# A three-stage attention and MoE kernel: small routing operations on GpSimd, three more DMA transposes per pair, own places for V's scale and smaller zero-fill pieces

## The chip, the core and the metric

The kernel runs on one core of one Trainium2 chip. The metric is the device time of one execution in microseconds (us). Three executions of the kernel before took 1109.99, 1111.71 and 1105.46 us; their median is 1109.99 us. The engines are called as in the profile: PE is TensorE, DVE is VectorE, ACT is ScalarE, POOL is GpSimd, SP is SyncE, which here only issues DMAs.

## What is computed

The reference, cut to what matters, runs three layers one after the other on 4 batches of 576 tokens:

```python
# attention, 4 batches, 8 heads, 576 tokens, head size 64
scores = scale * q @ k.T
scores = where(scores >= max(scores) - tau, scores, -1e9)
attn = softmax(scores)
x = attn @ v                                   # 2304 tokens x 512
# MoE, 8 experts, one expert per token
logits = (x / |x|) @ (emb / |emb|).T / tau
idx = argmax(logits); gate = softmax(logits)[idx]
x = gate * (relu(x @ w1[idx]) @ w2[idx])
# dense layer
out = softplus(x @ w_in) @ w_out
```

## The kernel before, in words

**Phase A** is the attention and the routing of the tokens to their experts; it fills the first 400 us or so. Phases B (experts) and C (dense layer) follow, and the change leaves them alone.

Phase A works through 144 chunks, 36 to a batch: a chunk is 128 query rows of one head against all 576 keys (the last four chunks of a batch are two heads with 64 rows each). For a chunk n, PE makes the scores (`emit_s`, L284 and L287), DVE takes the row maximum (`emit_max`, L294) and the mask (`emit_mask`, L299), and ACT the exponential (`emit_exp`, L310). From there two chunks are handled as a **pair**: ACT rounds the exponentials to fp16 (`emit_hi`, L324), POOL makes the fp16 rest (`emit_lo`, L83 on tile PST). Both halves have to be transposed before PE can multiply them by V: 18 blocks of 128 x 128 per pair. 10 of them go by one DMA transpose that SP issues (L335), 8 over PE into a PSUM bank (`emit_half`, L349), from where ACT and DVE copy them out in turn (`emit_land`, L357 and L359). Then PE multiplies by V (`emit_pv`, L382) and DVE scales the result (`emit_evac`, L398 to L408).

The order of the work is written out by hand. Every operation gets a time in steps, one step per chunk, the list is sorted by that time, and the instructions are issued in this order; each engine runs its own in order. `emit_s` of chunk n stands at step n, the DMA transpose of its pair at n + 3.7, the product with V at n + 10.8. Other work is put between by the same clock:

- **V's scale** (L220 to L247). The next batch's V is split in two fp16 parts after a scale by its largest value. ACT takes maxima (`max_v`, L208), PE turns them (`prep_v0`, L220), DVE makes a factor (`prep_v1`), PE spreads it over the partitions (`prep_vb`, L242), DVE copies it out (`prep_vc`, L247). Then ACT and POOL make the two parts head by head (`prep_v2` L256/L258, `prep_v3` L83 on tile vl). `prep_v0` and `prep_vb` use one PSUM bank, called xt, together with the routing's transposes (`route_t` L430, evacuated by `route_x` L440) and logits (`route_l` L451, `route_c` L456). The places are VP + 0.95 to VP + 2.18 with VP = 30.
- **Routing** (`inv_norm` L85 to L108, `route_pick`, `route_gate`, `route_rank`). The operations on 128 x 5 and 128 x 40 elements of one batch run as a Python generator that moves on by one operation each half step, some 20 steps in all, beside the next batch's chunks. All of them are on DVE but the exponential. At its end POOL scatters the 5 token tiles into the buckets in HBM (`route_out`, L567). The last batch is routed in a tail after the 144 chunks, whose order is a string of words (DRAIN).
- **Zero fill** (`zero_fill`, L151). The 8 expert buckets are filled with zeros from a zero tile in SBUF, one DMA of 645 KB from 64 partitions per expert, on SP's queue, every 5 steps from step 20.

Of the kernel before, what the change touches and what calls it, by code (L numbers as in the profile page):

```python
# [44 lines left out]
DRAIN = """P8 g0 a1 z1 l2 a1 H2 a1 a1 H1 D3 a1 t5 P7 P6 a1 t4 D1 u5 L2 t3 a1 P5 c2 z1 p0 b1 V9 b1 a1 u4 a1 u3 P4 b1 t1 V5 b1 z1 b1 u1 t2 a1 u2 a1 z1 b1 z1 z1 a1 P3 r3 b1 b1 a1 x3 q3 b1 P2 V3 a1 b1 a1 g1 d1 d1 a1 P1 V1 l3 d1 r4 g2 d1 c3 q4 p1 d1 x4 d1 e1 f1 d1 e1 l4 f1 d1 e1 f1 e1 f1 d1 f1 e1 c4 z1 d1 e1 p2 h1 d1 e1 f1 d1 e1 f1 h1 a1 d1 e1 f1 h1 d1 f1 h1 f1 h1 f1 h1 d1 e1 d1 e1 e1 f1 h1 h1 e1 f1 d1 e1 f1 d1 e1 h1 d1 f1 f1 h1 e1 d1 d1 h1 d1 h1 e1 d1 e1 f1 h1 d1 e1 f1 h1 h1 e1 f1 f1 h1 d1 f1 h1 d1 e1 f1 e1 e1 f1 d1 f1 d1 e1 d1 h1 e1 h1 b1 h1 a1 z1 b1 z1 f1 b1 h1 a1 z1 b1 e1 e1 e1 b1 a1 a1 a1 d1 e1 b1 e1 d1 d1 e1 d1 e1 d1 d1 e1 d1 d1"""  # L45
QK0, QKD, V0, VD, VP, VS, Z0, ZD = 12, 7, 15, 3, 30, 2, 20, 5
DQ, DZ, VG = (0, 0, 0, 0), 1, 1
# [13 lines left out]
def attention_moe_moe_kernel(ctx: ExitStack, tc, qT, kT, v, tau, emb, moe_tau, w1, w2, wi, wo, out):  # L61
# [20 lines left out]
    def combine(eng, out, a, b, op):  # L82
        eng.tensor_tensor(out=out, in0=a, in1=b, op=op)  # L83

    def inv_norm(r, ss, t):  # L85
# [64 lines left out]
    def zero_fill(zeros, e, i):  # L150
        (act, sp)[DZ].dma_start(out=bucket[e * NT:e * NT + CAP].rearrange("(p r) c -> p r c", r=ZR)[64 * i:64 * i + 64],  # L151
                      in_=zeros.unsqueeze(1).to_broadcast([64, ZR, ROW]))

    def phase_a():
        with ExitStack() as es:
# [312 lines left out]
            def route_pick(b, t0, t1):  # L468
# [35 lines left out]
            def route_rank(b, t0, t1, eq, oh, shift):  # L504
# [35 lines left out]
            def route_gate(b, t0, t1):  # L540
# [17 lines left out]
                dve.tensor_scalar(out=gt, in0=gt, scalar1=1e-9, scalar2=None, op0=ALU.add)  # L558
                yield
# [111 lines left out]
            def at(n, fn, *a):  # L671
                work.setdefault(n, []).append((fn, a))
# [3 lines left out]
            def soon(t, fn, *a):  # L676
                late.append((t, fn, a))
# [627 lines left out]
```

## Time and profile before

| | before |
|---|---|
| median of three executions | 1109.99 us |
| the profiled execution | 1109.21 us, span 1107.5 us |
| PE busy | 993.5 us, 90% |
| DVE busy | 733.4 us, 66% |
| ACT busy | 619.0 us, 56% |
| POOL busy | 548.6 us, 50% |
| mean granted TensorE clock | 0.957 of full speed |

The busy shares are means over three phases with different limits. How the time of phase A is spent can be read from windows (busy time of each engine in a chosen stretch), from the list of waits, and from the timeline. Times are counted from the start of the span.

### The profile page before, as it was taken

Reading aid. Unit: us, or ns where it says so; the run is one execution under the profiler, and the core shown is the slowest. Engines: PE = TensorE matmul, PEld = TensorE weight load, DVE = VectorE, ACT = ScalarE, POOL = GpSimd, SP = SyncE. Lnnn points to the kernel's source line nnn. Section 1 sums busy time; section 2 is a strip of 40 time slices with the busy share of each in tenths; the row PEclk is TensorE's granted clock in tenths of the full one; section 3 lists DMA queues with packets and bytes.
Section 4 is the critical chain, followed back from the end, with each engine's and each line's share of the span. In section 5 each row is a group of like instructions: output and inputs, shape, how many; then the busy total and the mean of one; then the engine's idle time right before and its main releaser. Section 6 shows DMA issues by size and latency. Waiting matters only on the chain. (4 is left out here: it accounts for less than half of the span.)

```text
span 1107.5 us, 19252 instructions
## 1 busy us (share of the span) xinstructions
PE 993.5 (90%) x7314; PEld 849.9 (77%) x7314; DVE 733.4 (66%) x1432; ACT 619.0 (56%) x1070; POOL 548.6 (50%) x426
## 2 busy tenths in 40 slices
PE   6777887988798869999999998988899999999997
PEld 4665765767676658999999897766688888898996
DVE  7876897789689874766776558888533443544543
ACT  6776966878596743444444434444544544444543
POOL 4644646555564721656445442211555565565652
PEclk9888998999899978999999999899999999999999
DMA  5675987457443646887878866421100010010000
GB/s 153 130 155 118 165 164 150 97 115 139 113 91 63 129 131 201 206 225 212 207 204 183 194 181 129 152 76 39 50 26 1 29 39 1 29 39 1 29 1 29
DMA packets 155462, 121.73 MB, mean 110 GB/s; under 512 B 102360, under 2 KB 127960, under 8 KB 155360
## 3 DMA queue, kind: packets, MB, share of 16 engines
q1 hardware_dynamic: 136416, 93.16, 37.0%
q10 hardware_dynamic: 16032, 17.78, 6.4%
q0 software_dynamic: 2912, 9.48, 2.3%
q8 instruction: 59, 0.97, 0.4%
q14 instruction: 43, 0.35, 0.1%
HBM read 75.05 MB, written 20.01 MB: 86 GB/s over the span
## 5 line engine op out<-in xcount | busy, mean ns | idle before, releaser
L83 POOL TENSOR_TENSOR PST<-E,PST 128x1152 f16<-128x1152 f32 (+1 forms) x74 | 169.8, 2296 | 169.8 <-ACT PST L324 111.7
L1185 PE MATMUL a<-wo,g 128*128 128x512 f32 x864 | 218.3, 399 | 9.4 <-DVE g L83 9.4
L1157 PE MATMUL ch_ps<-cxt,wi 128*128 128x512 f32 (+1 forms) x960 | 214.7, 372 | 5.2 <-DVE cxt L83 3.2
L1157 PEld LDWEIGHTS ch_ps<-cxt,wi 128*128 128x128 f32 x960 | 177.3, 190 | 34.6 <-DVE cxt L83 3.5
L1185 PEld LDWEIGHTS a<-wo,g 128*128 128x128 f32 x864 | 162.2, 189 | 49.0 <-DVE g L83 13.7
L83 POOL TENSOR_TENSOR t<-e,t 128x512 f32<-128x512 f32 (+1 forms) x78 | 92.8, 1189 | 203.5 <-DVE t L1169 203.5
L284 PE MATMUL S<-k,qz 128*128 128x288 f32 x512 | 163.1, 444 | 19.8 <-DVE ss L98 7.0
L294 DVE TENSOR_SCALAR_CACHE_REDUCE Sb<-S,tau_s 128x576 f32<-128x576 f32 x144 | 116.6, 810 | 60.8 <-PE S L284 35.7
L1169 DVE TENSOR_SCALAR t<-e 128x512 f32<-128x512 f32 (+1 forms) x80 | 33.7, 421 | 157.6 <-ACT e L1167 157.6
L932 PE MATMUL h_ps<-xt,w 128*128 128x320 f32 x768 | 128.9, 316 | 5.1 <-ACT w L791 2.3
L83 POOL TENSOR_TENSOR w<-st,w 128x1024 fp32r<-128x1024 f32 x30 | 73.5, 2450 | 118.0 <-ACT w L791 116.1
L1166 ACT ACTIVATE e<-ch_ps 128x512 f32<-128x512 f32 (+1 forms) x80 | 44.1, 551 | 154.2 <-PE ch_ps L1157 154.2
L948 PE MATMUL y<-h,w 128*128 128x320 f32 x768 | 123.2, 310 | 0.0
L932 PEld LDWEIGHTS h_ps<-xt,w 128*128 128x128 f32 x768 | 115.0, 189 | 9.6 <-DVE w L83 3.8
L284 PEld LDWEIGHTS S<-k,qz 128*128 128x128 f32 x512 | 92.0, 200 | 39.2 <-issue 14.8
L299 DVE SCALAR_TENSOR_TENSOR Sb<-S,th,Sb 128x576 f32<-128x576 f32 x144 | 117.8, 818 | 5.1
L948 PEld LDWEIGHTS y<-h,w 128*128 128x128 f32 x768 | 115.8, 189 | 0.0
L382 PEld LDWEIGHTS <-PT 128*128 128x128 f16 (+1 forms) x2240 | 89.9, 104 | 24.2 <-issue 4.9
L310 ACT ACTIVATE E<-Sb,nb 128x576 f32<-128x576 f32 x144 | 103.8, 768 | 6.6 <-POOL PST L83 0.4
L382 PE MATMUL pv<-vh,PT 128*128 128x65 f16 (+1 forms) x1440 | 98.1, 199 | 6.1 <-DMA vh<-vh 3.5
L83 POOL TENSOR_TENSOR g<-g,t 128x512 f32<-128x512 f32 (+1 forms) x62 | 87.0, 1404 | 4.9
L791 ACT ACTIVATE w<-st 128x1024 fp32r<-128x1024 f32 x64 | 67.5, 1055 | 34.3 <-DMA st<-in_w 24.1
(166 smaller groups left out, 1438.0 us busy)
## 6 DMA issues: line engine op xcount, KB each, us to landing
st<-in_w SPq DMA_DIRECT2D x64, 512.0 KB, 5.2
raw<-in_wi SPq DMA_DIRECT2D x16, 512.0 KB, 4.7
raw<-in_wo SPq DMA_DIRECT2D x16, 512.0 KB, 3.3
bucket<-qz SPq DMA_DIRECT2D x8, 645.0 KB, 6.1
yT<-y ACTq DMA_DIRECT2D x7, 640.0 KB, 9.0
vst<-in_v ACTq DMA_DIRECT2D x12, 320.0 KB, 3.7
xr<-bucket SPq DMA_DIRECT2D x7, 516.0 KB, 5.8
k<-in_kT ACTq DMA_DIRECT2D x12, 288.0 KB, 2.9
```

The lines of the kernel that those rows point to most:

```text
L83: eng.tensor_tensor(out=out, in0=a, in1=b, op=op)
L284: pe.matmul(st[:, f, 0:HALF], q[:, h // 2, o:o + 128], k[:, h // 2, fs])
L294: dve.tensor_scalar(out=Sb[n], in0=St[n][:, :, 0:HALF], scalar1=tau_s[:, 0:1], scalar2=None, op0=ALU.subtract, op1=ALU.max, accum_out=TH[g ...
L299: dve.scalar_tensor_tensor(out=Sb[n], in0=St.pop(n)[:, :, 0:HALF], scalar=TH[g][:, j:j + 1], in1=Sb[n], op0=ALU.is_lt, op1=ALU.subtract)
L310: act.activation(out=Et[g][:, i].rearrange("p (f k) -> p f k", f=2), in_=Sb.pop(g * GS + i), func=ACTF.Exp, scale=-SCALE, bias=nb[:, i:i + 1])
L382: pe.matmul(oo, l, r, start=(z == 0), stop=(z == len(mms) - 1))
L791: act.activation(out=hi, in_=src, func=ACTF.Copy)
L932: pe.matmul(hps[:, 0:CAP], a[:, c, 128 * (f % 2):128 * (f % 2) + 128], b[:, c], start=(z == 0), stop=(z == 11))
L948: pe.matmul(Y[e][c][:, 0:CAP], a[:, f % 2, 128 * c:128 * c + 128], b, start=(f == 0 and z == 0), stop=(f == 7 and z == 2))
L1157: pe.matmul(h, a[:, r:r + 128], x[:, c, 0:n], start=(z == 0), stop=(z == 11))
L1166: act.activation(out=e, in_=h, func=ACTF.Abs)
L1185: pe.matmul(A[b][t], a[:, 128 * t:128 * t + 128], x, start=(f == 0 and z == 0), stop=(f == 15 and z == 2))
```

## The change

It has five parts.

- Of a pair's 18 blocks 13 now go by DMA (NDMA) and 5 over PE; the copy out of PSUM is 640 columns instead of 1024.
- For the first three batches most of the small routing operations move from DVE to POOL. `inv_norm_pool` takes the place of `inv_norm`; where one DVE instruction did two operations, POOL needs two instructions: 17 POOL instructions per batch stand for 13 on DVE. Where another engine takes the result up, 5 half steps (PLAG) are put between, so that a batch's routing lasts 18 half steps longer.
- V's scale: the load of V moves from steps 15, 18, 21, 24 to 14, 16, 18, 20, the maxima from 22 to 28 to 17 to 23, and the scale's own four operations from 30.95, 31.18, 31.95, 32.18 to 26.05, 27.18, 28.85, 29.18. The two parts of V start at step 30 instead of 34.
- Zero fill in 32 pieces of 161 KB, each from 16 partitions, from step 12, every 1.5 steps.
- POOL's order at the end of phase A: as the routing lasts longer, the third batch's scatters come later.

```diff
-NDMA, TLAG = 10, 6
-RKY, RKZ, VM, VMD = 2, 3, 22, 2
-QK0, QKD, V0, VD, VP, VS, Z0, ZD = 12, 7, 15, 3, 30, 2, 20, 5
+NDMA, TLAG = 13, 6
+PLAG = 5
+RKY, RKZ, VM, VMD = 2, 3, 17, 2
+QK0, QKD, V0, VD, VP, VS, Z0, ZD = 12, 7, 14, 2, 26, 2, 12, 1.5
...
+    def inv_norm_pool(r, ss, t):
+        dve.tensor_scalar(out=r.bitcast(U32), in0=ss.bitcast(U32), scalar1=1, scalar2=None,
+                          op0=ALU.logical_shift_right)
+        yield
+        dve.tensor_scalar(out=r.bitcast(U32), in0=r.bitcast(U32), scalar1=-1.0, scalar2=float(0x5F3759DF),
+                          op0=ALU.mult, op1=ALU.add)
+        yield
+        yield
+        combine(pool, t, r, r, ALU.mult)
+        combine(pool, t, t, ss, ALU.mult)
+        yield
+        pool.tensor_scalar(out=t, in0=t, scalar1=-0.5, scalar2=1.5, op0=ALU.mult, op1=ALU.add)
+        combine(pool, r, t, r, ALU.mult)
...
+        pool.tensor_scalar(out=t, in0=t, scalar1=1e-6, scalar2=None, op0=ALU.add)
+        for _ in range(PLAG):
+            yield
+        dve.reciprocal(out=r, in_=t)
...
     def zero_fill(zeros, e, i):
-        ...[64 * i:64 * i + 64], in_=zeros.unsqueeze(1).to_broadcast([64, ZR, ROW]))
+        ...[16 * i:16 * i + 16], in_=zeros.unsqueeze(1).to_broadcast([16, ZR, ROW]))
...
-                pt = HT[g] = pr.tile([128, 1024], F16, tag="T", name="T")
+                pt = HT[g] = pr.tile([128, 1024], F16, tag="T", name="T")[:, 0:128 * (18 - NDMA)]
...
-                yield from inv_norm(nrm, SS[b][0:R, t0:t1], tmp)
+                yield from (inv_norm_pool if b < B - 1 else inv_norm)(nrm, SS[b][0:R, t0:t1], tmp)
...
+                side = pool if b < B - 1 else dve
...
-                    dve.tensor_tensor(out=lg, in0=lg, in1=mx.unsqueeze(2).to_broadcast(bc), op=ALU.subtract)
+                    side.tensor_tensor(out=lg, in0=lg, in1=mx.unsqueeze(2).to_broadcast(bc), op=ALU.subtract)
...
+                if side is pool:
+                    pool.tensor_scalar(out=eq, in0=lg, scalar1=0.0, scalar2=None, op0=ALU.is_ge)
+                    combine(pool, eq, eq, iota, ALU.mult)
...
-                    dve.tensor_tensor(out=runs[0:R], in0=runs[0:R], in1=sm1, op=ALU.add)
+                    combine(pool, runs[0:R], runs[0:R], sm1, ALU.add)
...
-                soon(s0 + VP + 0.95, prep_v0, b + 1)
+                soon(s0 + VP + 0.05, prep_v0, b + 1)
                 soon(s0 + VP + 1.18, prep_v1, b + 1)
-                soon(s0 + VP + 1.95, prep_vb, b + 1)
-                soon(s0 + VP + 2.18, prep_vc, b + 1)
+                soon(s0 + VP + 2.85, prep_vb, b + 1)
+                soon(s0 + VP + 3.18, prep_vc, b + 1)
...
-                for i in range(CAP // (64 * ZR)):
-                    at(Z0 + ZD * e + i, zero_fill, QZ[0][64:128, 0, 0:ROW], e, i)
+                for i in range(CAP // (16 * ZR)):
+                    at(int(Z0 + ZD * (4 * e + i)), zero_fill, QZ[0][64 + 16 * i:80 + 16 * i, 0, 0:ROW], e, i)
```

The change moves instructions at three places that matter below. New line numbers are larger by 1 to 48, since lines were added: L284 becomes L314, L382 becomes L412, L83 becomes L84.

PE, in the second batch, around the turning of V's maxima (tile vx_ps; S are scores, pv the products with V, T the transposes over PE). Before:

```order
L382 LDWEIGHTS PT
L382 MATMUL pv_2557<-vh_187,PT 128x65
L220 MATMUL vx_ps<-ident,vmx 4x128
L284 MATMUL S<-k,qz_120 128x288 x2
L349 LDWEIGHTS PST
L349 MATMUL T<-ident_117,PST 128x128
```

Now:

```order
L412 LDWEIGHTS PT
L412 MATMUL pv_2184<-vh_187,PT 128x65
L314 MATMUL S<-k,qz_120 128x288 x2
L250 MATMUL vx_ps<-ident,vmx 4x128
L412 LDWEIGHTS PT
L412 MATMUL pv_2325<-vh_185,PT 128x65
```

The turning stood ahead of the scores of chunk 31, so that these waited behind it. It now stands five chunks earlier and behind the scores of its step.

DVE, in the second batch, around the first steps of the first batch's inverse norm (nrm, tmp and ss are its tiles; Sb are the chunks' masks and maxima). Before:

```order
L89 TENSOR_SCALAR nrm<-nrm 128x5
L359 COPY PT<-T 128x1024
L92 TENSOR_TENSOR tmp<-nrm 128x5
L294 TENSOR_SCALAR Sb,th<-S,tau_s 128x576
L299 SCALAR_TENSOR_TENSOR Sb<-S,th,Sb 128x576
L94 SCALAR_TENSOR_TENSOR tmp<-tmp,ss 128x5
L96 SCALAR_TENSOR_TENSOR nrm<-tmp,nrm 128x5
L294 TENSOR_SCALAR Sb,th<-S,tau_s 128x576
L299 SCALAR_TENSOR_TENSOR Sb<-S,th,Sb 128x576
```

Now:

```order
L116 TENSOR_SCALAR nrm<-nrm 128x5
L389 COPY PT<-T 128x640
L324 TENSOR_SCALAR Sb,th<-S,tau_s 128x576
L329 SCALAR_TENSOR_TENSOR Sb<-S,th,Sb 128x576
L324 TENSOR_SCALAR Sb,th<-S,tau_s 128x576
L329 SCALAR_TENSOR_TENSOR Sb<-S,th,Sb 128x576
L486 COPY lg<-lg_ps 64x8
L324 TENSOR_SCALAR Sb,th<-S,tau_s 128x576
L329 SCALAR_TENSOR_TENSOR Sb<-S,th,Sb 128x576
L428 SCALAR_TENSOR_TENSOR rd<-pv_1887,vma 128x4
```

L92 to L106 are gone from DVE; what is left of the inverse norm there are its two first operations and, five half steps after POOL's last, the reciprocal.

POOL, from the last chunks to the end of phase A (bucket are the scatters; sm is the count of the third batch's tokens). Before:

```order
L570 MEMSET pad 1x1
L83 TENSOR_TENSOR PST<-E,PST 128x576
L567 DMA bucket<-xs,ix 18432x516
L570 MEMSET pad 1x1
L83 TENSOR_TENSOR PST<-E,PST 128x576
L567 DMA bucket<-xs,ix 18432x516
L570 MEMSET pad 1x1
L83 TENSOR_TENSOR PST<-E,PST 128x576
L567 DMA bucket<-xs,ix 18432x516
L570 MEMSET pad 1x1
L83 TENSOR_TENSOR PST<-E,PST 128x576 x3
L567 DMA bucket<-xs,ix 18432x516
```

Now:

```order
L84 TENSOR_TENSOR PST<-E,PST 128x576 x2
L602 TENSOR_SCALAR gt<-gt 128x5
L84 TENSOR_TENSOR PST<-E,PST 128x576 x4
L84 TENSOR_TENSOR runs<-runs,sm_5576 128x8
L615 DMA bucket<-xs,ix 18432x516
L618 MEMSET pad 1x1
L615 DMA bucket<-xs,ix 18432x516
L618 MEMSET pad 1x1
```

The third batch's five scatters stood between the last chunks' work. They now stand behind all of it, directly ahead of the last batch's five: ten in a row.

## Rows read from the trace of the kernel before

**Rows 1.** Windows, all engines: busy us and instructions, granted clock, DMA share, GB/s

```profile
106.20:133.90 27.70, 25.76 (x344) 21.05 (x343) 23.64 (x53) 26.92 (x48) 19.56 (x14) 1.00 0.95 158
139.10:179.10 40.00, 33.63 (x409) 27.02 (x405) 38.92 (x91) 30.10 (x53) 19.14 (x10) 0.96 0.92 169
179.10:203.60 24.50, 17.86 (x144) 14.08 (x145) 13.00 (x34) 11.91 (x19) 13.25 (x15) 0.72 0.41 105
236.10:275.80 39.70, 33.36 (x411) 26.96 (x407) 38.22 (x91) 30.29 (x53) 19.15 (x10) 0.96 0.76 140
```

**Rows 2.** Windows of L299 alone, one instruction per chunk: DVE busy (count), clock, DMA

```profile
106.20:133.90 27.70, 9.82 (x12) 1.00 0.95 158
139.10:179.10 40.00, 13.09 (x16) 0.96 0.92 169
179.10:203.60 24.50, 4.91 (x6) 0.72 0.41 105
275.80:299.30 23.50, 4.91 (x6) 0.78 0.42 106
332.00:371.00 39.00, 12.27 (x15) 0.96 0.36 65
81.10:106.20 25.10, 5.91 (x8) 0.80 0.56 113
```

**Rows 3.** Timeline of PE, 182 to 200 us: start, us, instruction [idle before <- releaser]

```profile
182.68 0.37 PE L220 MATMUL vx_ps<-ident,vmx 128*4 128x128 f32 x1 [3.62 <-ACT xt L440]
...
187.63 0.38 PE L242 MATMUL vb_ps<-vmd,ones 4*128 4x4 f32 x2 [1.51 <-DVE vmd L233]
...
191.33 1.87 PE L451 MATMUL lg_ps<-enT,xt 128*128 128x8 f32 x8 [1.17 <-DVE vma L247]
```

**Rows 4.** Waits, 60 to 395 us, PE's: us in total, times, longest us

```profile
PE vx_ps L220 <- ACT xt L440: 11.8, 3, 4.6
...
PE T L349 <- ACT PT L357: 9.7, 13, 1.8
```

**Rows 5.** Groups by line and form, DVE: busy us, mean ns, idle before

```profile
L94 DVE SCALAR_TENSOR_TENSOR tmp<-tmp,ss 128x5 f32<-128x5 f32 x3 | 6.7, 2248 | 0.0
...
L493 DVE SCALAR_TENSOR_TENSOR eq<-lg,iota 128x40 f32<-128x40 f32 x3 | 3.5, 1154 | 0.0
...
L106 DVE TENSOR_SCALAR tmp<-tmp 128x5 f32<-128x5 f32 x3 | 3.1, 1028 | 0.0
...
L532 DVE TENSOR_TENSOR runs<-runs,sm 128x8 f16<-128x8 f16 x3 | 2.1, 711 | 0.0
...
L96 DVE SCALAR_TENSOR_TENSOR nrm<-tmp,nrm 128x5 f32<-128x5 f32 x3 | 0.5, 167 | 0.1
```

**Rows 6.** Timeline of POOL and DVE: the same two engines within one stretch

```profile
146.87 2.37 POOL L83 TENSOR_TENSOR PST<-E,PST 128x1152 f16<-128x1152 f32 x1 [3.71 <-ACT PST L324]
...
147.01 2.25 DVE L94 SCALAR_TENSOR_TENSOR tmp<-tmp,ss 128x5 f32<-128x5 f32 x1
```

**Rows 7.** Groups by line and form: copies of transposed blocks out of PSUM

```profile
L357 ACT ACTIVATE PT<-T 128x1024 f16<-128x1024 f16 x34 | 34.0, 1001 | 0.0
...
L359 DVE COPY PT<-T 128x1024 f16<-128x1024 f16 x34 | 23.1, 679 | 1.5 <-PE T L349 1.5
...
L615 ACT ACTIVATE PT<-pt_ps 128x640 f16<-128x640 f16 x5 | 3.4, 696 | 4.7 <-PE pt_ps L609 4.7
```

**Rows 8.** DMA issues: KB each, median us from issue to landing

```profile
bucket<-qz SPq DMA_DIRECT2D x8, 645.0 KB, 6.1
...
PT<-PST SPq DMA_TRANSPOSE x71, 4.0
```

**Rows 9.** Timeline of POOL and DVE at the end of phase A

```profile
400.79 0.98 POOL L567 DMA_INDIRECT bucket<-xs,ix  x1 [9.69 <-DVE nrm L89]
...
406.36 0.90 POOL L567 DMA_INDIRECT bucket<-xs,ix  x1 [0.22 <-DVE off L977]
...
417.56 0.48 DVE L899 TENSOR_SCALAR xr<-xr 64x512 f32<-64x512 f32 x1 [0.34 <-DMA xr<-bucket]
```

More of the change, by code (lines that the diff above doesn't have):

```diff
@@ L109, in inv_norm @@
         yield
+    def inv_norm_pool(r, ss, t):
[12 more added lines that the diff above has]
+        yield
+        combine(pool, ss, r, ss, ALU.mult)
+        combine(pool, t, ss, r, ALU.mult)
+        yield
+        pool.tensor_scalar(out=r, in0=t, scalar1=0.375, scalar2=-1.25, op0=ALU.mult, op1=ALU.add)
+        combine(pool, r, r, t, ALU.mult)
+        yield
+        pool.tensor_scalar(out=r, in0=r, scalar1=1.875, scalar2=None, op0=ALU.add)
+        combine(pool, t, r, ss, ALU.mult)
+        yield
+        pool.tensor_scalar(out=t, in0=t, scalar1=1e-6, scalar2=None, op0=ALU.add)
+        for _ in range(PLAG):
+            yield
+        dve.reciprocal(out=r, in_=t)
+        yield
     def setup_early(rt):
@@ L150, in zero_fill @@
     def zero_fill(zeros, e, i):
-        (act, sp)[DZ].dma_start(out=bucket[e * NT:e * NT + CAP].rearrange("(p r) c -> p r c", r=ZR)[64 * i:64 * i + 64],
-                      in_=zeros.unsqueeze(1).to_broadcast([64, ZR, ROW]))
+        (act, sp)[DZ].dma_start(out=bucket[e * NT:e * NT + CAP].rearrange("(p r) c -> p r c", r=ZR)[16 * i:16 * i + 16],
+                      in_=zeros.unsqueeze(1).to_broadcast([16, ZR, ROW]))
     def phase_a():
@@ L482, in route_pick, with lag @@
                 oh = new("oh", F16)
+                side = pool if b < B - 1 else dve
+                def lag():
+                    for _ in range(PLAG if b < B - 1 else 0):
+                        yield
                 def shift():
-                    dve.tensor_tensor(out=lg, in0=lg, in1=mx.unsqueeze(2).to_broadcast(bc), op=ALU.subtract)
+                    side.tensor_tensor(out=lg, in0=lg, in1=mx.unsqueeze(2).to_broadcast(bc), op=ALU.subtract)
                 dve.tensor_reduce(out=mx, in_=lg, axis=AX.X, op=ALU.max)
@@ L492, in route_pick @@
                     yield
-                dve.scalar_tensor_tensor(out=eq, in0=lg, scalar=0.0 if T > 1 else mx[:, 0:1], in1=iota, op0=ALU.is_ge,
-                                         op1=ALU.mult)
+                if side is pool:
+                    pool.tensor_scalar(out=eq, in0=lg, scalar1=0.0, scalar2=None, op0=ALU.is_ge)
+                    combine(pool, eq, eq, iota, ALU.mult)
+                else:
+                    dve.scalar_tensor_tensor(out=eq, in0=lg, scalar=0.0 if T > 1 else mx[:, 0:1], in1=iota,
+                                             op0=ALU.is_ge, op1=ALU.mult)
                 yield
+                yield from lag()
                 dve.tensor_reduce(out=im, in_=eq, axis=AX.X, op=ALU.min)
@@ L545, in route_gate @@
                 if T > 1:
-                    dve.tensor_tensor(out=ex, in0=LG[b][0:R, t0:t1],
-                                      in1=RP.pop((b, t0)).unsqueeze(2).to_broadcast(bc), op=ALU.mult)
+                    combine(pool if b < B - 1 else dve, ex, LG[b][0:R, t0:t1],
+                            RP.pop((b, t0)).unsqueeze(2).to_broadcast(bc), ALU.mult)
+                    for _ in range(PLAG if b < B - 1 else 0):
+                        yield
                     act.activation(out=ex, in_=ex, func=ACTF.Exp)
@@ L557, in route_gate @@
                     yield
-                dve.tensor_scalar(out=gt, in0=gt, scalar1=1e-9, scalar2=None, op0=ALU.add)
+                if b < B - 1:
+                    pool.tensor_scalar(out=gt, in0=gt, scalar1=1e-9, scalar2=None, op0=ALU.add)
+                    for _ in range(PLAG):
+                        yield
+                else:
+                    dve.tensor_scalar(out=gt, in0=gt, scalar1=1e-9, scalar2=None, op0=ALU.add)
                 yield
```

## The prediction

> **What bounds the kernel now.** Phases B and C are untouched, so only the first 400 us can change, and a mean busy share says nothing about them. I read windows of all engines first, then the count of chunks in the same windows, then the timeline of the slow ones, then single instructions.
>
> The windows show three kinds of stretch in every batch [rows 1]. In the first (106.2 to 133.9 us) ACT is busy for 26.92 of 27.70 us: there ACT splits the next batch's V. In the second (139.1 to 179.1 us) DVE is busy for 38.92 of 40.00 us: there the routing's small operations run between the chunks. [...] The counts give the pace [rows 2]: 12 chunks in 27.7 us (2.31 us per chunk), 16 in 40.0 (2.50), 6 in 24.5 (4.08). The third kind comes back at 275.8 us (6 chunks in 23.5 us) and, longer at its front, at 81.1 us (8 chunks in 25.1 us).
>
> In that third stretch the timeline of PE shows three waits in a row [rows 3]: 3.62 us for ACT's evacuation of bank xt before V's maxima are turned, 1.51 us for DVE's factor, 1.17 us for DVE's copy that frees the bank again. The scores of the next chunk stand behind each of them, so DVE, ACT and POOL run dry, and after PE's waits the clock falls. Over three batches the first of these waits alone is 11.8 us [rows 4].
>
> In the DVE-bound stretch some operations on five elements are far longer than their size: L94 takes 2248 ns, L493 1154, L106 1028, L532 711, while L96 on the same shape takes 167 [rows 5]. The timeline shows why: L94 starts at 147.01 us and ends at 149.26, POOL's subtraction runs from 146.87 to 149.24 [rows 6]. DVE ends when POOL does.
>
> **The change, part by part**, against the profiled execution (1109.2 us; the median of the three is 0.8 us above it).
>
> *V's scale on steps of its own.* At the ACT-bound pace (2.31 us) the three slow stretches would take 13.9, 13.9 and 18.5 us, so they hold 10.6 + 9.6 + 6.6 = 26.8 us of excess. I take that pace, not a faster one, because the split of V now begins at step 30 and so lies in this stretch. The operation that PE waited for stood 1.05 steps ahead of the turning; now the last of the maxima stands 2.15 steps ahead, and the wait of 3.62 us shrinks by 1.1 x 2.31 = 2.5 us to about 1.1 us. The bank is free by then (the logits' copy stands before the turning), and the factor has more than a step. Worth 26.8 - 3 x 1.1 = 23.5 us; the bounds are 26.8 and, if the first wait stays whole, some 12 us.
>
> *Small operations on POOL.* Off DVE per batch go the four long ones, 2.25 + 1.15 + 1.03 + 0.71 = 5.14 us, and nine short ones at about 0.167, 1.50 us: 6.6 us, in three batches 19.9. L86 (the shift) stays and can still be caught by POOL. ACT is no cap: it is busy for fewer us than DVE there. The DMA engines may be one. Their share is 0.92 in the first such stretch, 0.76 in the second, 0.36 in the third [rows 1, 2]. The last gives the price of a DMA transpose, there nearly the only traffic: 0.36 x 39.0 / 7.5 pairs = 1.9 us of DMA time, so three more blocks cost 0.56 us per pair. Eight pairs add 4.5 us: 36.8 + 4.5 = 41.3 us in the first stretch, which leaves no gain, 30.2 + 4.5 = 34.7 of 39.7 in the second, up to 5.0 us, and no cap in the third. I take 0.5 + 5.0 + 6.6 = 12 us; the bounds are 0 and 19.9.
>
> On POOL 17 small instructions per batch come in between the subtractions. POOL is busy for 19.14 of 40.00 us in that stretch [rows 1], so its own time is covered. What is not: DVE takes up POOL's result three times per batch, and ACT once. If POOL is late it is late by up to one subtraction, 2.37 us [rows 6]; nothing to 21 us over nine such places. I take one per batch, 7 us. [...]
>
> *13 blocks by DMA.* The copy shrinks from 1024 to 640 columns. On ACT that is 1.00 us against 0.70 for a copy of 640 columns of the same kind [rows 7], once per four chunks; on DVE 0.68 us against something between 0.42 (in proportion) and 0.68, I take 0.48. In three ACT-bound stretches of 12 chunks 2.7 us, in three DVE-bound ones of 16 chunks 2.4 us, together 5. PE's three transposes less per pair give nothing by themselves: PE waits for others in all three stretches. The T bank's waits for ACT (9.7 us [rows 4]) may shorten too; counted in the 5. The landing of a transpose, 4.0 us [rows 8], grows in proportion to at most 5.2.
>
> *Zero fill in 32 pieces, and the DMA engines as a whole.* The pieces carry the same bytes, with less to stand behind on SP's queue. But the share is 0.95 and 0.92 in the two stretches with the fill [rows 2]; six pairs add 3.4 us to 26.3 of 27.7. So 0 to some 4 us, and V's loads now have three steps, 7 us, before ACT wants them. I take 4 us lost.
>
> *The end of phase A.* The third batch's five scatters now stand ahead of the last batch's five. Five take from 400.79 to 407.26 us, 6.5 us [rows 9], and the experts' first rows wait for the last one: DVE's L899 at 417.56 is released by that load. The added five can begin about 1.5 us before 400.79, when their indices are ready. 5 us lost, between 0 and 6.5.
>
> Sum: 23.5 + 12 + 5 - 7 - 4 - 5 = 24.5 us. 1109.2 - 24.5 = 1084.7, and with the 0.8 us to the median **1085 us**. Where the stall in the third stretch goes, ACT is the next that is late: it has the split of V on its hands there.
>
> **The rivals.**
>
> [...]
>
> *The change of places does not do what it says:* the turning of the maxima now waits for ACT's last maximum, and half the stall stays. 12 us more than forecast, 1097 us. For it: ACT's queue also holds the loads' issues. Against: the reckoning above.
>
> *Nothing stands in the way:* no wait for POOL, no cap by DMA. 23.5 + 19.9 + 5 - 5 = 43 us, 1067 us.
>
> *POOL becomes the hub, and the kernel gets slower.* The routing ends 9 steps later, so a batch's five scatters fall into the steps in which POOL also makes V's second part. A scatter of 1.3 us and half a subtraction of 2.37 are 2.5 us per chunk, over the pace of 2.31. Then the DMA transposes start late, PE waits, and the clock falls: a stretch at 4.08 us per chunk stays, only moved, and every taking-up costs 2.37 us. Price: the 23.5 us are gone, 21 instead of 7 lost: 12 + 5 - 21 - 4 - 5 = -13, 1122 us. It decides where POOL's idle time before its subtractions is gone for a whole stretch. Against: POOL is idle for half of the DVE-bound stretch and nearly half of the third.
>
> **How the numbers follow.** My forecast 0.48, DMA as the bound 0.20, half the stall stays 0.12, nothing in the way 0.12, POOL as the hub 0.08. The three executions differ by 0.5%, so about that much can be told from no change: faster is below 1104.4 us, slower above 1115.5. The forecast and the third rival are faster, the first and second mostly, the last is slower: 0.84 faster, 0.08 same, 0.08 slower. The range reaches from the case in which nothing is in the way to the upper end of the DMA case: 1066 to 1106 us.
>
> **What would show it.** Right: the stretch before each batch's end takes about 2.3 us per chunk with a clock near 1; PE's wait for V's maxima is about 1 us; DVE's sum in the routing stretch falls by about 6 us per batch; the first expert rows are ready 5 us later counted from the last chunk. Wrong: a new wait of DVE for POOL, of PE for PT, or of ACT for V's load in the list of waits, or a slow stretch somewhere else in the batch.

## The result and the profile after

The changed kernel takes 1095.81 us (median of four runs, 1093.78 to 1096.67) against 1108.72 for the kernel before: a ratio of 0.9881, with a 95% interval of 0.9848 to 0.9915. It is 1.2% faster. Forecast were 1085 us, so the saving is 12.9 us and not 24.5.

I cut each profiled execution at the same four places: the start of the last of the 144 chunks' maxima on DVE (end of the main loop), the first matmul into h_ps (start of the experts), the first into ch_ps (end of the experts), the end. These are the four stretches of the kernel before (columns as in [rows 1]).

```profile
0.00:385.60 385.60, 312.95 (x3514) 250.30 (x3515) 312.82 (x714) 290.08 (x491) 211.50 (x169) 0.92 0.63 127
385.60:422.60 37.00, 24.89 (x362) 23.22 (x358) 23.11 (x109) 13.97 (x28) 10.29 (x16) 0.77 0.57 173
422.60:679.10 256.50, 247.39 (x1620) 237.31 (x1620) 171.20 (x228) 116.85 (x191) 126.08 (x66) 0.99 0.75 196
679.10:1107.50 428.40, 408.30 (x1824) 339.10 (x1824) 226.22 (x382) 198.05 (x361) 200.70 (x177) 0.98 0.13 38
```

And of the changed kernel (profiled at 1093.78 us, span 1092.1):

```profile
0.00:356.80 356.80, 292.81 (x3287) 231.13 (x3288) 289.65 (x671) 280.42 (x491) 219.96 (x212) 0.94 0.80 154
356.80:396.50 39.70, 25.57 (x386) 23.64 (x382) 22.19 (x114) 14.16 (x28) 13.63 (x23) 0.77 0.47 150
396.50:663.90 267.40, 251.83 (x1621) 241.01 (x1621) 175.90 (x228) 116.64 (x192) 126.42 (x66) 0.98 0.76 192
663.90:1092.10 428.20, 407.94 (x1824) 338.80 (x1824) 226.04 (x382) 197.96 (x361) 200.56 (x177) 0.98 0.12 38
```

The main loop lost 28.8 us. The end of phase A became 2.7 us longer, and the experts' stretch 10.9 us longer (256.5 to 267.4), although no instruction in it is touched by the change. The rest is the same to 0.2 us.

Inside the main loop, windows of the changed kernel from one batch's routing into the next batch:

```profile
133.30:172.60 39.30, 31.66 (x358) 24.27 (x355) 33.35 (x79) 30.95 (x55) 22.87 (x26) 0.96 1.12 209
172.60:184.70 12.10, 11.73 (x144) 9.65 (x142) 11.75 (x30) 9.76 (x20) 7.72 (x6) 0.97 0.45 87
184.70:198.20 13.50, 7.48 (x81) 5.80 (x80) 5.81 (x16) 8.88 (x16) 7.02 (x6) 0.75 0.65 130
```

DVE's one instruction per chunk (L329 now) counts the chunks in the last two:

```profile
172.60:184.70 12.10, 4.91 (x6) 0.97 0.45 87
184.70:198.20 13.50, 2.46 (x3) 0.75 0.65 130
```

The third stretch of [rows 1] (6 chunks in 24.5 us at a clock of 0.72) is gone: 6 chunks in 12.1 us at 0.97. But right behind it 3 chunks now take 13.5 us, at 0.75 (1.00 from 184.7 to 190.3 us, 0.50 from 190.4 to 197.1). The list of PE's waits (60 to 375 us) says why:

```profile
PE rk_ps L565 <- ACT xt L470: 11.5, 2, 6.0
PE pv L412 <- DMA PT<-PST: 7.5, 6, 3.1
...
PE vx_ps L250 <- DVE lg L486: 1.0, 3, 0.5
```

The wait for V's maxima, 11.8 us before [rows 4], is 1.0. In its place PE waits twice some 6 us for the routing's rank matmul. The wait for the transposes by DMA (tile PT) has grown too; before, over 60 to 390 us, it was

```profile
PE pv L382 <- DMA PT<-PST: 2.6, 2, 2.0
```

The timeline of PE shows what stands ahead of the rank matmul,

```profile
186.18 0.63 PE L460 MATMUL xt_ps<-ident,xs 128*128 128x128 f32 x4
...
192.84 0.17 PE L565 MATMUL rk_ps<-oh,tri 128*128 128x8 f16 x1 [6.02 <-ACT xt L470]
```

and that of ACT when the bank was emptied:

```profile
190.57 0.68 ACT L387 ACTIVATE PT<-T 128x640 f16<-128x640 f16 x1
191.15 1.15 ACT L354 ACTIVATE PST<-E 128x1152 f16<-128x1152 f32 x1
192.21 0.58 ACT L470 ACTIVATE xt<-xt_ps 128x512 f32<-128x512 f32 x1
```

The rank uses PSUM bank xt. In the kernel before it stood ahead of the next batch's first transposes on that bank. The lags that wait for GpSimd moved it nine steps later, right behind such transposes, and ACT, which in that place empties the bank some 6 us after PE filled it, does so only when the work ahead in its queue is done.

The single instructions came out as forecast, first DVE's and then ACT's copy of the transposed blocks (128 x 640 for 128 x 1024 in [rows 7]; columns as there), with GpSimd's add to `runs`, which took DVE 711 ns in [rows 5]:

```profile
L389 DVE COPY PT<-T 128x640 f16<-128x640 f16 x30 | 14.4, 480 | 0.0
...
L387 ACT ACTIVATE PT<-T 128x640 f16<-128x640 f16 x34 | 23.1, 680 | 0.0
...
L84 POOL TENSOR_TENSOR runs<-runs,sm 128x8 f16<-128x8 f16 x3 | 0.6, 201 | 13.1 <-PE rk_ps L565 13.1
```

The DMA issues of the main loop, as in [rows 8]: pieces a quarter as large land hardly sooner (5.8 us for 6.1), and the transposes land later (4.9 us for 4.0).

```profile
bucket<-qz SPq DMA_DIRECT2D x32, 161.2 KB, 5.8
PT<-PST SPq DMA_TRANSPOSE x71, 4.9
```

At the end of phase A ten scatters stand in a row on POOL, where [rows 9] had five:

```profile
372.01 1.11 POOL L615 DMA_INDIRECT bucket<-xs,ix  x1 [3.43 <-DVE nrm L90]
...
385.90 0.90 POOL L615 DMA_INDIRECT bucket<-xs,ix  x1 [0.22 <-issue]
```

### The profile page after: what moved, and what is told of

It is laid out like the page before. It is cut to its first block, busy times and chain, and to the rows that moved or that the text cites. A ratio compares the mean times of both kernels' runs of the same rounds, so it can differ in the third digit from the quotient of the medians.

```text
span 1092.1 us, 18861 instructions
## 1 busy us (share of the span) xinstructions
PE 978.2 (90%) x7110; PEld 834.6 (76%) x7110; DVE 713.8 (65%) x1393; ACT 609.2 (56%) x1070; POOL 560.6 (51%) x477
## 5 line engine op out<-in xcount | busy, mean ns | idle before, releaser
L84 POOL TENSOR_TENSOR PST<-E,PST 128x1152 f16<-128x1152 f32 (+1 forms) x74 | 169.1, 2287 | 117.4 <-ACT PST L354 80.3
L84 POOL TENSOR_TENSOR t<-e,t 128x512 f32<-128x512 f32 (+1 forms) x78 | 92.6, 1187 | 203.5 <-DVE t L1217 203.5
L314 PE MATMUL S<-k,qz 128*128 128x288 f32 x512 | 166.2, 451 | 8.7 <-ACT k L216 3.5
L980 PE MATMUL h_ps<-xt,w 128*128 128x320 f32 x768 | 133.2, 323 | 12.7 <-ACT w L839 8.3
L84 POOL TENSOR_TENSOR w<-st,w 128x1024 fp32r<-128x1024 f32 x30 | 74.5, 2482 | 121.8 <-ACT w L839 121.6
L980 PEld LDWEIGHTS h_ps<-xt,w 128*128 128x128 f32 x768 | 118.5, 195 | 18.2 <-ACT w L839 9.9
L329 DVE SCALAR_TENSOR_TENSOR Sb<-S,th,Sb 128x576 f32<-128x576 f32 x144 | 117.8, 818 | 5.1
L314 PEld LDWEIGHTS S<-k,qz 128*128 128x128 f32 x512 | 93.8, 204 | 27.8 <-issue 5.0
L412 PEld LDWEIGHTS <-PT 128*128 128x128 f16 (+1 forms) x2240 | 87.2, 103 | 28.8 <-DMA PT<-PST 10.3
L412 PE MATMUL pv<-vh,PT 128*128 128x65 f16 (+1 forms) x1440 | 96.0, 197 | 10.8 <-DMA PT<-PST 7.5
L84 POOL TENSOR_TENSOR g<-g,t 128x512 f32<-128x512 f32 (+1 forms) x62 | 87.0, 1404 | 4.9
```

What stands on the lines that cost most here:

```text
L314: pe.matmul(st[:, f, 0:HALF], q[:, h // 2, o:o + 128], k[:, h // 2, fs])
L329: dve.scalar_tensor_tensor(out=Sb[n], in0=St.pop(n)[:, :, 0:HALF], scalar=TH[g][:, j:j + 1], in1=Sb[n], op0=ALU.is_lt, op1=ALU.subtract)
L412: pe.matmul(oo, l, r, start=(z == 0), stop=(z == len(mms) - 1))
L980: pe.matmul(hps[:, 0:CAP], a[:, c, 128 * (f % 2):128 * (f % 2) + 128], b[:, c], start=(z == 0), stop=(z == 11))
```

## The experiments

The rivals at this point. **A**: the rank's new place is a loss of its own. **B**: ACT is behind anyway, and the wait would only move. For the experts' stretch: either something in the change lengthens it, or it varies by itself. The table has the four stretches of each kernel's profiled execution, in us, then the median of all its runs and the ratio to the kernel before. Each ratio is taken against runs of the kernel before that were made beside it (their medians lie between 1108.49 and 1111.05 us). There is one profile per kernel; single runs of one kernel lie up to 15 us apart, so a stretch that differs by less than about 5 us from another kernel's says little alone.

| kernel | main loop | to the experts | experts | rest | median | ratio, 95% interval |
|---|---|---|---|---|---|---|
| before | 385.6 | 37.0 | 256.5 | 428.4 | 1108.72 | 1 |
| the change | 356.8 | 39.7 | 267.4 | 428.2 | 1095.81 | 0.9881, 0.9848 to 0.9915 |
| 1 rank early | 349.5 | 35.7 | 264.4 | 428.4 | 1078.65 | 0.9728, 0.9675 to 0.9781 |
| 2 ten blocks | 361.1 | 41.4 | 256.0 | 428.3 | 1091.43 | 0.9841, 0.9801 to 0.9882 |
| 3 small ops on DVE | 367.0 | 35.0 | 265.8 | 428.5 | 1099.35 | 0.9923, 0.9891 to 0.9955 |
| 4 V's steps alone | 369.7 | 35.8 | 255.9 | 428.4 | 1091.05 | 0.9851, 0.9794 to 0.9907 |
| 5 rank early, ten | 345.7 | 37.0 | 254.2 | 429.4 | 1067.87 | 0.9621, 0.9589 to 0.9653 |
| 6 rank early, twelve | 344.1 | 36.3 | 273.9 | 428.4 | 1080.80 | 0.9707, 0.9649 to 0.9764 |
| 7 rank early, eight pieces | 336.1 | 34.7 | 266.7 | 428.5 | 1073.33 | 0.9674, 0.9647 to 0.9701 |
| 8 thirteen alone | 378.5 | 36.6 | 273.4 | 428.4 | 1121.83 | 1.0111, 1.0083 to 1.0139 |
| 9 rank early, ten, eight pieces | 345.5 | 37.2 | 257.6 | 428.2 | 1070.53 | 0.9651, 0.9613 to 0.9690 |
| 10 thirteen, both ways | 342.8 | 37.1 | 261.1 | 428.2 | 1072.29 | 0.9677, 0.9628 to 0.9725 |
| 11 thirteen, then ten | 338.6 | 37.7 | 256.5 | 428.2 | 1062.82 | 0.9573, 0.9549 to 0.9598 |
| 12 ten, then thirteen | 343.4 | 36.4 | 260.7 | 429.7 | 1074.45 | 0.9698, 0.9661 to 0.9735 |

**1. The rank two chunks earlier.** RKN is the number of half steps between the routing's norm and its pick.

```diff
-RKN, SUN, SU0 = 4, 0, 12
+RKN, SUN, SU0 = 0, 0, 12
```

> The changed kernel with RKN 4 -> 0 alone: the rank of batches 0 to 2 stands two chunks earlier on TensorE, ahead of the next batch's xs transposes on the same PSUM bank and no longer right behind them. Theory A (the two chunks of 9.5 and 9.0 us, where the rank matmul waits 6 us for ScalarE to empty that bank, are a loss of their own, made by the lags that put the rank there): both chunks fall to 2 to 3 us, the main loop (to the start of the last chunk's max, 356.8 us in the changed kernel) ends at 341 to 345, the whole run takes 1079 to 1085 us. Rival B (ScalarE was behind anyway, and the wait only moves to the next op on that bank): the main loop stays within 4 us of 356.8, the run at 1092 to 1098. The 267 us of the experts' stretch (256.5 before) should not depend on this edit: near 267 again if the change caused it in another way, near 257 or anywhere between if it varies by itself.

The run came to 1078.65 us, 0.35 us under A's range. The two groups of chunks are repaired: the two chunks behind the V stretch take 3.3 us in both batches (11.1 and 10.5 in the changed kernel). B has fallen. The main loop missed its number, 349.5 against 341 to 345, since chunks 50 to 66 now take 45.1 us (39.3 in the changed kernel). There PE waits for a transpose's landing, and SP's queue shows that the transpose was issued late and long (timelines of PE, then of SP's queue; SPq rows are DMA issues):

```profile
157.46 0.24 PE L412 MATMUL pv<-vh,PT 128*128 128x65 f16 x1 [3.75 <-DMA PT<-PST]
```

```profile
145.86 3.17 SPq L365 DMA_TRANSPOSE PT<-PST  x1
149.08 1.04 SPq L181 DMA_DIRECT2D bucket<-qz  x1
150.24 5.23 SPq L365 DMA_TRANSPOSE PT<-PST  x1
155.51 2.17 SPq L181 DMA_DIRECT2D bucket<-qz  x2
```

**2. Ten blocks in place of 13.**

```diff
-NDMA, TLAG = 13, 6
+NDMA, TLAG = 10, 6
```

> The changed kernel with NDMA 13 -> 10 alone, so 8 blocks of a pair go over TensorE again. Theory (the 13 blocks gain what was forecast, 5 us, most of it the three transposes and the shorter eviction on TensorE and ScalarE): main loop 3 to 7 us longer, the run 1098 to 1104 us. Rival (the longer DMA transposes, issued late between the zero-fill pieces, take back what TensorE saves): within 2 us of 1096, and the waits for PT<-PST (7.5 us in all in the changed kernel) fall below 3.

Neither as a whole. The main loop did get 4.3 us longer, as the theory has it, and the waits for PT<-PST fell to 0.7 us, as the rival has it. But the run is 4 us faster (1091.43), because the experts' stretch is back at 256.0 us:

```profile
402.50:658.50 256.00, 247.71 (x1621) 237.75 (x1621) 168.52 (x228) 116.11 (x191) 125.14 (x66) 0.99 0.77 199
```

**3. The small operations back on DVE**, without their lags (all PLAG loops are empty).

```diff
-yield from (inv_norm_pool if b < B - 1 else inv_norm)(nrm, SS[b][0:R, t0:t1], tmp)
+yield from inv_norm(nrm, SS[b][0:R, t0:t1], tmp)
...
-side = pool if b < B - 1 else dve
+side = dve
...
-combine(pool, runs[0:R], runs[0:R], sm1, ALU.add)
+combine(dve, runs[0:R], runs[0:R], sm1, ALU.add)
```

> The changed kernel with the small routing ops of batches 0 to 2 back on VectorE and without their lags, V's steps, the 13 blocks and the 32 zero pieces kept. Theory A (the ops off VectorE gain 12 us in the main loop, and the lags then lose about 16 us at the rank): main loop 352 to 358, the run 1090 to 1098 us, with no chunk of 9 us. Rival B (the ops on VectorE cost nothing, since TensorE and ScalarE set the pace there too): the main loop ends at 340 to 344, the run at 1078 to 1085 us. Rival C (the ops off VectorE are worth more, 20 us): the run over 1099.

1099.35 us is just over the limit from which C was to hold, by less than its own runs differ (1097.46 to 1105.35); the main loop, 367.0, is 9 us over A's range. B has fallen. With experiment 1 as the other end, the small operations off DVE are worth 17.5 us of main loop when the rank doesn't stall (367.0 - 349.5), and 10.2 when it does.

**4. V's new steps alone**, in the kernel before.

```diff
-RKY, RKZ, VM, VMD = 2, 3, 22, 2
+RKY, RKZ, VM, VMD = 2, 3, 17, 2
...
-QK0, QKD, V0, VD, VP, VS, Z0, ZD = 12, 7, 15, 3, 30, 2, 20, 5
+QK0, QKD, V0, VD, VP, VS, Z0, ZD = 12, 7, 14, 2, 26, 2, 20, 5
```

> The kernel before with V's new steps alone (V0, VD, VP, VM and the four offsets of the scale's preparation), everything else as before. Forecast's term: 23.5 us less in the main loop, which then ends at 360 to 364 (385.6 before), the run at 1083 to 1088 us. Rival (half of the stall returns at the new place): main loop 370 to 376, the run 1093 to 1100. If the experts' stretch is longer by something in the change other than V's steps it is 255 to 259 us here, as before.

Between the two, nearer to the rival: the main loop is 15.9 us shorter, the run 1091.05. The experts' stretch is as before. Windows of this kernel's routing stretch and V stretch (16 and 6 chunks) show both halves:

```profile
133.60:178.90 45.30, 34.97 (x406) 27.87 (x403) 40.86 (x95) 32.38 (x54) 19.11 (x10) 0.92 0.77 156
178.90:191.30 12.40, 11.72 (x152) 9.69 (x149) 12.01 (x28) 10.45 (x20) 11.04 (x13) 1.00 0.53 132
```

The V stretch takes 12.4 us where it took 24.5 [rows 1], a gain of 12.1, more than forecast. But the routing stretch went from 40.0 to 45.3 us, since the maxima are turned there now and DVE, which must first finish, is late. The timeline of DVE,

```profile
161.94 2.27 DVE L498 TENSOR_TENSOR oh<-iota,im 128x40 f16<-128x40 f32 x1
...
166.12 0.19 DVE L552 TENSOR_REDUCE gt<-ex 128x5 f32<-128x40 f32 x1
```

that of PE behind it, and its row in the list of waits:

```profile
166.35 0.37 PE L220 MATMUL vx_ps<-ident,vmx 128*4 128x128 f32 x1 [2.97 <-DVE gt L552]
```

```profile
PE vx_ps L220 <- DVE gt L552: 5.8, 2, 3.0
```

A routing operation of 40 elements that took 544 ns on average before took 2.27 us here, and PE waits 2.97 us for DVE where it had waited 3.62 for ACT [rows 3].

**5 and 6. Rank early, with 10 and with 12 blocks.** Experiment 1 with this, and in 6 with a 12 in its place:

```diff
-NDMA, TLAG = 13, 6
+NDMA, TLAG = 10, 6
```

> The first experiment's kernel (rank two chunks earlier) with NDMA 13 -> 10. Theory C (the 13 blocks save about 4 us in the main loop and lose about 10 us in the experts' stretch, which they do not touch: 267.4, 264.4 and 265.8 us in the three kernels with 13 blocks so far, 256.5, 255.9 and 256.0 in the three with 10): main loop 348 to 355 us, experts 255 to 258 us, the run 1069 to 1076 us. Rival D (that split of the experts' stretch is chance): experts 262 to 268 us, the run 1079 to 1084 us.

> The first experiment's kernel with NDMA 13 -> 12. If the experts' stretch grows with the blocks that went by DMA, it is 260 to 264 us here and the run 1073 to 1078 us; if only some numbers of blocks lengthen it (as an arrangement of the DMA engines that a transfer leaves behind would), it is either 255 to 258 us, with the run at 1068 to 1073, or 264 to 268, with the run at 1077 to 1081. Main loop 349 to 353 us in all cases.

With 10 the run takes 1067.87 us and the experts 254.2: C, and a little better. With 12 the experts take 273.9 us, above every bracket, and the median is 1080.80. So the stretch does not seem to grow in step with the number of blocks: 10 is short, and 12 and 13 are both long. The profiled run with 12 was the slowest of its four (1071.16 to 1084.44).

**7. Rank early, with the zero fill of the kernel before.**

```diff
-at(int(Z0 + ZD * (4 * e + i)), zero_fill, QZ[0][64 + 16 * i:80 + 16 * i, 0, 0:ROW], e, i)
+at(Z0 + ZD * e + i, zero_fill, QZ[0][64:128, 0, 0:ROW], e, i)
```

(with Z0, ZD = 20, 5, and 64 partitions in `zero_fill`)

> The first experiment's kernel with the zero fill of the kernel before: 8 pieces of 64 partitions, five chunks apart, in place of 32 of 16 partitions every 1.5 chunks. Theory E (the small pieces keep the transposes' transfers short): main loop 4 to 8 us longer than 349.5, the run 1082 to 1087 us, with a wait of TensorE for PT of 3 us or more at each of the 8 pieces. Rival F (many small pieces crowd the SP queue, on which a transpose's issue took 2.5 to 5.2 us between them and 1.4 us elsewhere, and no fewer bytes move): main loop 3 to 8 us shorter, the run 1070 to 1076 us. Neither: within 3 us of 1078.7. The experts' stretch stays at 264 to 267 us if the 13 blocks make it long.

F: the main loop falls by 13.4 us to 336.1, the shortest of all, and the run to 1073.33. 9.7 of the 13.4 are chunks 50 to 66, which take 35.4 us. The profiled run was the fastest of its four (1067.75; the others 1072.33 to 1075.19).

**8. 13 blocks alone**, in the kernel before.

```diff
-NDMA, TLAG = 10, 6
+NDMA, TLAG = 13, 6
...
-pt = HT[g] = pr.tile([128, 1024], F16, tag="T", name="T")
+pt = HT[g] = pr.tile([128, 1024], F16, tag="T", name="T")[:, 0:128 * (18 - NDMA)]
```

> The kernel before with NDMA 10 -> 13 and the T tile cut to 5 blocks, nothing else. Theory C: main loop 379 to 383 us (385.6 before), experts 264 to 268 us (256.5 before), the run 1111 to 1116 us, so no gain at all. Rival D (the experts' stretch is not the blocks' doing): 255 to 258 us there, the run 1101 to 1106 us, as the forecast's 5 us had it.

C, and by more: the main loop is 7.1 us shorter, the experts' stretch 16.9 us longer (columns as above),

```profile
415.10:688.50 273.40, 255.50 (x1620) 244.05 (x1620) 176.40 (x228) 116.96 (x191) 124.91 (x66) 0.96 0.73 184
```

and the kernel is 1.1% slower. By itself this part of the change is a loss.

**9. Rank early, 10 blocks, 8 pieces**: experiment 7 with one more line.

```diff
-NDMA, TLAG = 13, 6
+NDMA, TLAG = 10, 6
```

> The first experiment's kernel with 10 blocks and the 8 zero pieces of the kernel before, so V's steps and the small ops on GpSimd are all that is kept of the change, with the rank two chunks earlier. If the parts add up (the pieces lose about 10 us in the main loop, the 13 blocks save 2 to 5 us there and lose about 10 in the experts' stretch): main loop 336 to 343 us, experts 254 to 257 us, the run 1056 to 1065 us, the fastest of all. Rival (with 10 blocks the 32 pieces cost nothing, since a shorter transpose fits between them): main loop 344 to 347 us, the run 1065 to 1070 us as in the fifth experiment.

The rival: 345.5 us of main loop against 345.7 with 32 pieces, 1070.53 us against 1067.87. With 10 blocks the pieces make no difference. Windows of one batch (chunks 72 to 108), first of experiment 4 and then of this one, give the small operations their price:

```profile
191.30:283.10 91.80, 78.52 (x934) 63.41 (x933) 80.00 (x184) 74.39 (x126) 54.47 (x41) 0.94 0.63 125
```

```profile
183.80:266.80 83.00, 73.52 (x936) 59.72 (x932) 72.70 (x170) 73.69 (x127) 58.05 (x58) 1.00 0.68 140
```

DVE is busy 7.3 us less (80.00 to 72.70), and the batch is 8.8 us shorter. Windows from 60 us on, of experiment 5 (32 pieces, the first four issued before 60 us) and of this one (8), show the load on the DMA engines (the last three columns are clock, DMA share and GB/s):

```profile
60.00:184.10 124.10, 106.83 (x1315) 86.78 (x1316) 106.38 (x242) 106.09 (x181) 72.70 (x58) 0.99 0.90 155
```

```profile
60.00:183.80 123.80, 107.37 (x1315) 87.49 (x1315) 104.26 (x238) 104.57 (x178) 71.99 (x58) 0.97 0.84 157
```

The share has other traffic in it. The fill can be picked out, since up to 195 us its packets alone are of 2064 bytes, 2560 in each kernel. Summed over the trace, they take 34.2 us of all 16 engines in experiment 5 and 26.7 here. In the seven kernels with 32 pieces they take 29.4 us (the change) to 34.2, in the seven with 8 pieces 23.2 to 26.7 (26.5 in the kernel before).

**10. 13 blocks by DMA, and TensorE transposes 8 all the same.** Three of the blocks that TensorE makes are left in PSUM unread; nothing else of the computation changes.

```diff
-for a in range(NDMA, 9 * GS):
+for a in range(NDMA - 3, 9 * GS):
...
-act.activation(out=o, in_=HT.pop(g), func=ACTF.Copy)
+act.activation(out=o, in_=HT.pop(g)[:, 384:], func=ACTF.Copy)
```

> The first experiment's kernel (13 blocks by DMA) in which TensorE transposes 8 blocks all the same; the three that have come by DMA too are left in PSUM unread. DMA traffic, ScalarE's and VectorE's work are those of 13 blocks, TensorE's program is that of 10. If the longer experts' stretch comes from what the transposes' traffic leaves on the DMA side, it is 264 to 274 us here as in the five kernels with 12 or 13; if it comes from TensorE's side (length and place of its program), it is 254 to 257 us. Main loop 350 to 356 us (349.5 and up to 4.5 more for 71 x 3 transposes).

261.1 us lies in neither bracket, nearer to the lower end of the first. The main loop, 342.8 us, is below what was expected: the collision of experiment 1 in chunks 50 to 66 did not come about. TensorE's program was that of 10 blocks, and the stretch is still longer than in any kernel with 10, but only by 3.5 us. So this speaks against the length of TensorE's program and does not exclude it. The 213 idle transposes did not lengthen the run (1072.29; experiment 1 had 1078.65).

**11 and 12. 13 blocks in batches 0 to 2 and 10 in batch 3, and the other way round**, both with the rank early and 8 pieces: experiment 7 with a function of the pair g in the place of NDMA. In 11 it is this; in 12 the two numbers change places.

```diff
+def nd(g):
+    return 13 if g < 54 else 10
```

> The seventh experiment's kernel (rank early, 8 zero pieces) with 13 blocks by DMA for the pairs of batches 0 to 2 and 10 for those of batch 3. If the experts' stretch is lengthened by the transposes that stand just ahead of it, it is 254 to 258 us here, the main loop 336 to 341, and the run 1055 to 1063 us, the fastest of all; if by all that went before (three quarters of the extra blocks are still there), it is 261 to 270 us and the run 1065 to 1075 us.

> The complement: 10 blocks for the pairs of batches 0 to 2 and 13 for those of batch 3, with the rank early and 8 zero pieces. If what stands just ahead counts, the experts take 264 to 270 us and the run 1074 to 1082 us; if all that went before (a quarter of the extra blocks), 256 to 260 us and the run 1066 to 1072 us. Main loop 342 to 345 us.

Experiment 11 is the fastest of all, 1062.82 us, and falls where the first case had it: main loop 338.6, experts 256.5. In 12 the median, 1074.45, is in the first case's range; the profiled run was the fastest of its four, and its experts' stretch, 260.7, is just above the second case's range. So 10 blocks in the last batch are enough for a short stretch, and experiment 12, which lies between, agrees with that only by its median. One row in ACT's list of waits is that for weights (us in total, times, longest), here in the kernel before, the changed one and experiment 11:

```profile
ACT w L791 <- DMA st<-in_w: 20.7, 12, 5.4
```

```profile
ACT w L839 <- DMA st<-in_w: 28.9, 12, 7.3
```

```profile
ACT w L842 <- DMA st<-in_w: 25.2, 14, 4.0
```

The longest wait for a weight piece is 4.0 to 5.4 us in the six kernels with 10 blocks ahead of the experts, and 5.0 to 7.7 us in the eight others; the totals are 20.7 to 28.0 and 24.3 to 32.9 us. Both ranges overlap, so this is one place where the longer stretch is felt, and no proof. The granted clock is lower too: 0.96 over the whole stretch in experiment 8, 0.99 before.

Is the split chance, with one profile per kernel? An estimate from all runs says no: if a run that takes longer than the profiled one does so in the experts' stretch, the medians put that stretch at 254.0 to 258.9 us in the six kernels and at 262.4 to 276.6 in the eight.

## Why the prediction was right or wrong

The main loop was forecast to lose 29.5 us (24.5, and the 5 of the end) and lost 28.8. That agreement is luck: errors of both signs cancel. A chain of kernels that differ by one part each splits it: before to experiment 4, V's steps, -15.9; to 9, the small operations with the rank out of the way, -24.2; to 7, 13 blocks, -9.4; to 1, 32 pieces, +13.4; to the change, the rank's place, +7.3. Gains of 49.5 us and losses of 20.7; forecast were 40.5 (23.5 + 12 + 5) and 11 (7 + 4).

The two losses depend on the order of the chain. 9.7 of the 13.4 us are the collision in chunks 50 to 66, and it is not the same in every kernel with 32 pieces: these chunks take 45.1 us in experiment 1, 39.3 in the change, 36.1 and 36.2 in experiments 6 and 10, against 35.4 with 8 pieces (experiment 7). The chunks behind the rank's place (72 to 86 and 108 to 122) get 10.4 us shorter from the change to experiment 1 and 11.2 from experiment 2 to 5. So in the changed kernel itself the rank costs some 10 us in these chunks, and the collision some 4, about what was forecast for the pieces.

*V's scale, 23.5 us: right in place, wrong as a part.* The three stretches did not shrink by 23.5 us but, already in experiment 4, by 9.3, 12.1 and 11.1, together 32.5, since the last two run at 2.07 us per chunk and not at the 2.31 that I took from ACT's stretch. One reading behind the sum was wrong too: the window of 25.1 us from 81.1 us holds 7 whole chunks and the end of an eighth (5.91 us of DVE in [rows 2], where 8 chunks would be 6.55), so its excess at 2.31 us was 8.9 us and not 6.6. The step that failed is "the factor has more than a step", which looked only at the place that the work left. The place that it went to is the routing stretch, then full on DVE: 5.3 and 6.3 us came back there in two batches, and the rest of the 16.6 (32.5 - 15.9) in smaller amounts elsewhere. That is the rival "half the stall stays" by another engine: 5.8 us of waits for DVE in place of 11.8 for ACT. Only with the small operations off DVE does it vanish.

*Small operations, 12 us with bounds of 0 and 19.9: too small.* They are worth 24.2 us beside V's steps (with the rank out of the way), over the upper bound, and 17.5 beside 13 blocks and 32 pieces, where the collision of experiment 1 takes part of it. DVE's 6.6 us per batch were counted from the kernel before; with V's work in the same stretch they became 7.3, and PE's waits for DVE went with them. The cap by the DMA engines, which took the gain of the first stretch, was no cap: chunks 50 to 66 went from 45.3 us to 37.9 with 10 blocks, and with 13, where the sum had 41.3 us, they take 39.3 in the change and 35.4 in experiment 7. The share in the change's row of this stretch is 1.12: the packets' times add up to more than the 16 engines' time, so adding them to a share near 1 gives no bound. POOL was not the faster place by itself: in the changed kernel an operation on 128 x 5 or 128 x 8 takes 0.20 to 0.25 us there, and one that nothing disturbs took 0.167 on DVE [rows 5]. It is not what decided.

*Waits for POOL, 7 us: not there.* No wait of DVE or ACT for POOL stands in their lists over the main loop; the lags cover it. But the lags have a price that I did not count, though I wrote that the routing ends nine steps later: the rank's place on bank xt. Moving it back shortens the main loop by 7.3 us with 13 blocks and by 15.4 with 10 (experiments 2 and 5), and the order of the two kernels' instructions showed it before any run.

*13 blocks, 5 us: right for the main loop, and the wrong sign for the kernel.* The copies are 480 and 680 ns long, as taken, and the main loop gains 4.3, 7.1 and 9.4 us in three pairs of kernels (the change and 2, before and 8, 7 and 9); in a fourth (1 and 5) it loses 3.8, in the collision with the zero pieces. "Phases B and C are untouched, so only the first 400 us can change" is the sentence that failed: with 12 or 13 blocks ahead of it the experts' stretch takes 260.7 to 273.9 us in eight kernels, with 10 it takes 254.2 to 257.6 in six. Alone, the part makes the kernel slower (experiment 8). Why is open. It is not the zero pieces (7 and 8 have 8, and are long). The length of TensorE's program and the bytes alone are unlikely (experiment 10; 12 blocks are no better than 13), each on the word of one kernel. How transposes by DMA lengthen a stretch that follows them, no run showed.

*Zero pieces, 4 us: between 0 and 13.* With 10 blocks nothing (345.5 and 345.7), with 13 up to 13.4 us, when a transpose's issue is stuck between pieces (5.23 us in experiment 1). The fill's packets take 34.2 us of all engines in experiment 5 and 26.7 in experiment 9, so the pieces of 16 partitions cost 28% more; in the kernel before and the change it is 26.5 and 29.4. The chance of 0.20 for DMA as the bound and the range's upper end, 1106 us, rest on a term that no run shows, a fill of twice its DMA time; the runs show 28% more (5 and 9) and 11% more (before and the change). The fill's own time could be estimated from the kernel before: two of the eight fills add 0.16 of DMA share to a stretch of 40.0 us [rows 1], so all of them 26 us, against the 26.5 measured.

*End of phase A, 5 us: 2.7 measured, not shown as a part.* With all ten scatters behind the main loop and the rank early this stretch takes 34.7 to 37.7 us (eight kernels), with five 35.0 to 37.0 (before, 3, 4 and 8). Only with the rank late is it longer (39.7 and 41.4).

Faster was the likeliest class, the range held the time, and the sign was right. But the forecast of 1085 us was missed by 10.8 us, and two of its signs of being wrong came: PE's wait for PT grew from 2.6 to 7.5 us, and a slow stretch stood elsewhere in the batch. The 1097 us of the rival "half the stall stays" is nearest in number, but the stall that it kept is gone; what took its place was in no rival: a bank's turn in the main loop, and a stretch that nobody touched.

## What to carry to other kernels

A lag that hides one engine's latency also moves everything behind it: read the new order for what the moved work now stands behind, bank by bank, before counting the lag as free. Work that is moved out of a stall goes into another stretch, so ask what that stretch is full of. A part is not worth the same in every company: 32 pieces cost nothing beside 10 blocks and up to 13.4 us beside 13. And measure each part over the whole span: one part of this change paid in its own stretch and cost more in one that it did not touch. With the rank moved, the pieces left as they were and that part kept away from the untouched stretch, the gain of 1.2% became 4.3% (experiment 11).

## What was not expected of the hardware

The experts' stretch depends on how many blocks the transposes before it moved by DMA: 254.2 to 257.6 us after 10 per pair in the last batch, 260.7 to 273.9 after 12 or 13, with the same instructions in it; the cause is open. On SP's queue the issue of a transpose in the changed kernel took 1.49 us (median) outside the zero fill and 2.62 us within it; in experiment 1 one took 5.23 us, and the next issue on that queue began 0.04 us after it ended. And a five-element operation (L94) is 2.25 us long on DVE while POOL runs a subtraction of 2.37 us [rows 6]; the two instructions that stand for it on POOL take about 0.20 us each.
